# Token blocks of 512, 384 and 320 in place of 512, 480 and 320, in a fused attention and two-layer MLP kernel

## The chip, the cores and the metric

The kernel runs on one core of one Trainium2 chip. The metric is the device time of one execution in microseconds. A core has five engines with a queue of instructions each: TensorE (PE, matmuls), VectorE (DVE), ScalarE (ACT), GpSimd (POOL) and SyncE (SP, which issues nearly all DMA transfers here).

## The reference

Tokens `x` (12480 x 128, fp32) pass an induced-set attention with 32 inducing points, and then two MLP layers of width 2048. All is fp32.

```python
def mab(q, kv):
    s = scale * (q @ kv.transpose(0, 2, 1))
    s = s - s.max(-1, keepdims=True)
    a = np.exp(s)
    a /= a.sum(-1, keepdims=True) + 1e-09
    return a @ kv
h = mab(I, x)            # 32 x 128, over all tokens
x = mab(x, h)            # 12480 x 128

h = x @ w_in             # layer 1: 128 -> 2048
r = np.maximum(h, 0.0)
x = (s * (r * r) + b) @ w_out

h = x @ w_in2            # layer 2: 128 -> 2048
g = np.where(h >= 1, h, np.where(h <= -1, 0.0, (h + 1) ** 2 / 4))
out = g @ w_out2
```

## The kernel before

The tokens are cut into 25 blocks (`SIZES`): 20 of 512 tokens, four of 480 and one of 320. Tokens lie in a block as rows by parts: a block of `n` tokens is loaded as `n / 4` partitions with four tokens each (`KB = 4`), so a block of 480 is a load of 120 partitions and one of 320 a load of 80.

**First attention (the ramp).** Blocks go in groups of four (`g` = 0 to 6; group 5 holds blocks 20 to 23, group 6 block 24). SP loads them (`load_x`, tile `xc`). A group whose blocks have 120 rows is loaded as 112 rows for each block (L310) and one piece with the last 8 rows of all four (L308). PE transposes each block (`ptr`, L327), ACT copies it out (`x`, through a helper at L252), PE makes the scores of the four blocks side by side in one PSUM tile (`psc`, L344), DVE keeps a running maximum (`mx`, `m`, L350 to L358), ACT takes the exp (`e`, L364), PE transposes it (`pe`, L389), ACT copies (`eT`), and PE multiplies with the tokens (`ph`, L400) into the running sum `hsum`. `finish` makes `hT` of it, the 32 points of the second attention. Between these steps stands the conversion of the MLP weights, which come as 64-bit numbers (`raw_in`, `raw_out`, 512 KB a piece) and are made fp32 by ACT (`cvs`, an abs, L460) and DVE, and are then split in a high and a low fp32r part. Fillers (`warm`, `idle`) keep PE at work in planned gaps. SP's DMA instructions carry the waits of eight semaphores in turn, so each waits until the one eight places ahead has landed.

**Main loop.** A block has eight steps of two 128-wide slices of the hidden layer (`SPB = 8`, `GW = 2`); 25 blocks make 200 steps. A step `t` does layer 1 for step `t` and layer 2 for step `t - 18` (`LAG`). On PE it has 20 matmuls with the block's token count as columns: two of `in1` (`h`, L706), six of `out1` (`y`, L763 to L765), six of `in2` (`h`, L802 to L804) and six of `out2` (`y`, L763 to L765). Layer 1: ACT takes relu and square (L721, L728), POOL splits (`hi` L256, `lo` L738). Layer 2: DVE clips (`cl`, L809), ACT squares (L813), DVE adds (L820), ACT makes `hi` (L252), DVE makes `lo` (L830). `h2`, the PSUM tile of `in2`, has two buffers, and `lo` reads it, so `in2` of a step waits for `lo` of two steps before. At a block's end the result is transposed by DVE (`o`, L856) and stored by four DMAs (L860).

**Order.** The instructions of the ramp are emitted in the order of a list (`JOBS`) and of times that a planner (`Plan`) gives them by a table of costs. From step 26 to 192 the order is fixed by `ORDER`. From step 193 on the order comes from the list `LAST` (a letter is an operation, the number a step counted from 182), again through the planner; `EH` and `EL` set the engine of `hi` and `lo` for steps 175 to 181, and `TH` and `TL` for steps 182 to 199 (A is ACT, D is DVE, P is POOL). The last four steps of the last block skip the split and use a plain fp32 product (`out2_whole`, L847).

**Second attention.** For the MLP's input the scores of a group of up to four blocks (`sizes`) are taken with `hT` (L623), transposed by DVE, and turned into a softmax over some ten small operations of DVE, POOL and ACT that stand in the main loop, ahead of the blocks that need them.

Of the kernel before, what the change touches and what calls it, by code (L numbers as in the profile page):

```python
# [1306 lines left out]
```

## Time and profile before

| | |
|---|---|
| median of 3 runs | 940.8 us (938.71 to 940.96) |
| profiled execution | 942.43 us |
| its span in the trace | 940.6 us |
| PE busy | 921.8 us (98%) |
| ACT, DVE, POOL busy | 839.8, 808.3, 749.1 us |
| DMA | 28.13 MB moved; the packets of the main queue take 11.7% of the time of 16 engines |

The span is the time from the first to the last event of the core; the rest of the execution's time lies around it. The busy time of an engine is the time in which at least one of its instructions ran. Matmuls are pipelined and their ends are modelled, so what a matmul costs is read from the distance of the starts. "Idle before" stands in brackets behind an instruction, with what released it. The granted clock of PE is given as a share: 1.00 is 2.4 GHz and 0.50 is 1.2 GHz.

### The profile page before, as it was taken

The numbers are of one execution on the slowest core, as the hardware profiler recorded it, in microseconds if no ns is written. First come the engines' busy times: TensorE is split into PE (matmuls) and PEld (weight loads), VectorE is DVE, ScalarE is ACT, GpSimd is POOL, SyncE is SP. The second block draws the span as 40 slices with busy tenths as digits, with TensorE's granted clock in tenths as the row PEclk, the third lists the DMA queues.
The fourth block names the chain that finished last, engine by engine and source line by source line (L and its number), as shares of the span: only waits on it lengthen the run. The fifth ranks groups of instructions, "written<-read, shape, count | busy, mean of one in ns | idle before, by whom it ended". The sixth has DMA issues, their size and how long they took to land.

```text
span 940.6 us, 12488 instructions
## 1 busy us (share of the span) xinstructions
PE 921.8 (98%) x4540; PEld 779.7 (83%) x4540; DVE 808.3 (86%) x835; ACT 839.8 (89%) x911; POOL 749.1 (80%) x508
## 2 busy tenths in 40 slices
PE   8899999999999999999999999999999999999997
PEld 6654588888888888888888888888888888998986
DVE  6788988888898888898888888889888889888996
ACT  5658899999999999999999999999999999998874
POOL 0011389998999989999999899889999888997884
PEclk9999999999999999999999999999999999999999
DMA  9613000020001000002000002000110000000001
GB/s 336 207 45 90 0 1 13 12 45 12 1 12 43 15 12 12 1 11 53 7 9 12 7 5 46 12 1 12 20 35 12 11 1 13 19 1 11 11 12 18
DMA packets 64630, 28.13 MB, mean 30 GB/s; under 512 B 53224, under 2 KB 57992, under 8 KB 64568
## 3 DMA queue, kind: packets, MB, share of 16 engines
q1 hardware_dynamic: 64240, 27.28, 11.7%
q8 instruction: 36, 0.59, 0.3%
q14 instruction: 26, 0.21, 0.1%
q10 hardware_dynamic: 328, 0.04, 0.0%
HBM read 14.80 MB, written 6.39 MB: 23 GB/s over the span
## 4 chain that ended last, share of the span: by engine, by line
PE 92%; DMA 2%; ACT 2%; DVE 2%; issue 1%; SPq 0%; POOL 0%; ACTq 0%; DVEq 0%
PE y L763 17%; PE y L764 17%; PE y L765 17%; PE h L802 9%; PE h L804 9%; PE h L803 9%; PE h L706 9%; PE y L776 3%; DMA raw_out<-in_moe_w_out_dram 1%; DMA raw_in<-in_moe_w_in_dram 1%; ACT g L721 1%; ACT g L728 1%; PE ph L400 1%; DMA xc<-in_x_dram 0%; PE y L847 0%
## 5 line engine op out<-in xcount | busy, mean ns | idle before, releaser
L738 POOL TENSOR_TENSOR lo<-g,hi 128x1024 fp32r<-128x1024 f32 (+2 forms) x182 | 425.8, 2339 | 15.2
L809 DVE TENSOR_SCALAR cl<-h 128x1024 f32<-128x1024 f32 (+2 forms) x200 | 238.9, 1196 | 80.0 <-PE h L804 78.9
L763 PE MATMUL y<-hi,wout 128*128 128x512 f32 (+2 forms) x756 | 284.1, 376 | 0.9 <-DVE o L856 0.9
L764 PE MATMUL y<-lo,wout 128*128 128x512 f32 (+2 forms) x756 | 283.1, 374 | 0.3 <-POOL lo L830 0.3
L765 PE MATMUL y<-hi,wout 128*128 128x512 f32 (+2 forms) x756 | 282.9, 374 | 0.0
L813 ACT ACTIVATE cl<-cl,mhalf 128x1024 f32<-128x1024 f32 (+2 forms) x200 | 225.6, 1128 | 44.5 <-DVE cl L809 43.2
L256 POOL TENSOR_SCALAR hi<-g 128x1024 fp32r<-128x1024 f32 (+2 forms) x182 | 187.4, 1030 | 54.0 <-PE y L765 50.1
L820 DVE SCALAR_TENSOR_TENSOR h<-h,cl 128x1024 f32<-128x1024 f32 (+1 forms) x175 | 213.6, 1221 | 11.6 <-ACT cl L813 1.8
L830 DVE TENSOR_TENSOR lo<-h,hi 128x1024 fp32r<-128x1024 f32 (+1 forms) x175 | 211.9, 1211 | 8.0 <-ACT hi L252 7.6
L728 ACT ACTIVATE g<-g 128x1024 f32<-128x1024 f32 (+2 forms) x199 | 205.6, 1035 | 5.4
L721 ACT ACTIVATE g<-h 128x1024 f32<-128x1024 f32 (+2 forms) x198 | 195.2, 986 | 3.4 <-PE h L706 3.4
L252 ACT CAST hi<-h 128x1024 fp32r<-128x1024 f32 (+1 forms) x175 | 174.1, 995 | 1.3 <-DVE h L820 1.3
L763 PEld LDWEIGHTS y<-hi,wout 128*128 128x128 f32 x756 | 142.8, 189 | 22.4 <-issue 3.9
L764 PEld LDWEIGHTS y<-lo,wout 128*128 128x128 f32 x756 | 142.9, 189 | 18.0 <-POOL lo L830 0.7
L765 PEld LDWEIGHTS y<-hi,wout 128*128 128x128 f32 x756 | 142.9, 189 | 17.9
L802 PE MATMUL h<-y,win 128*128 128x512 f32 (+2 forms) x400 | 151.5, 379 | 1.8 <-DVE lo L830 1.2
L803 PE MATMUL h<-y,win 128*128 128x512 f32 (+2 forms) x400 | 149.5, 374 | 0.0
L804 PE MATMUL h<-y,win 128*128 128x512 f32 (+2 forms) x400 | 149.5, 374 | 0.0
L706 PE MATMUL h<-qt,hw 128*128 128x512 f32 (+2 forms) x400 | 119.8, 384 | 1.2 <-ACT g L721 0.9
L706 PEld LDWEIGHTS h<-qt,hw 128*128 128x128 f32 x400 | 74.9, 189 | 17.8 <-issue 4.7
L802 PEld LDWEIGHTS h<-y,win 128*128 128x128 f32 x400 | 75.5, 189 | 16.5 <-DVE lo L830 4.5
L804 PEld LDWEIGHTS h<-y,win 128*128 128x128 f32 x400 | 75.6, 189 | 9.5
(146 smaller groups left out, 648.1 us busy)
## 6 DMA issues: line engine op xcount, KB each, us to landing
xc<-in_x_dram SPq DMA_DIRECT2D x20, 256.0 KB
out_dram<-o SPq DMA_DIRECT2D x80, 64.0 KB
qin<-x SPq DMA_DIRECT2D x76, 64.0 KB
raw_in<-in_moe_w_in_dram SPq DMA_DIRECT2D x8, 512.0 KB
raw_out<-in_moe_w_out_dram SPq DMA_DIRECT2D x8, 512.0 KB
qin<-x SPq DMA_DIRECT2D x16, 60.0 KB
out_dram<-o SPq DMA_DIRECT2D x16, 60.0 KB
xc<-in_x_dram SPq DMA_DIRECT2D x4, 224.0 KB
```

The costliest lines, as they stand in the source:

```text
L706: nc.tensor.matmul(turned(p[:, j, :tb(bl)], bl), hw[f // 4][:, (f % 4) * 128:(f % 4 + 1) * 128], turns(qt[bl], bl), start=True, stop=True)
L728: nc.scalar.activation(g1[t], g1[t], AF.Square)
L738: engine[eng].tensor_sub(lo1[t], g1.pop(t), hi1[t].bitcast(F32))
L763: nc.tensor.matmul(p, whi, mhi, start=first, stop=False)
L764: nc.tensor.matmul(p, whi, mlo, start=False, stop=False)
L765: nc.tensor.matmul(p, wlo, mhi, start=False, stop=last)
L802: nc.tensor.matmul(o, whi, mhi, start=True, stop=False)
L803: nc.tensor.matmul(o, wlo, mhi, start=False, stop=False)
L804: nc.tensor.matmul(o, whi, mlo, start=False, stop=True)
L809: nc.vector.tensor_scalar(cl[t][:, part(js)], h2[t][:, part(js), :tb(t // SPB)], -1.0, 1.0, op0=ALU.max, op1=ALU.min)
L813: nc.scalar.activation(k, k, AF.Square, bias=mhalf, scale=0.5)
L820: nc.vector.scalar_tensor_tensor(oo[t][:, part(js)], h, -1.0, cl[t][:, part(js)], op0=ALU.max, op1=ALU.add)
```

## The change

The blocks become 23 of 512 tokens, one of 384 (block 23) and one of 320 (block 24). `SPAN` says how many partitions the last two are loaded to: 128 with three tokens each, and 64 with five each. The load of group 5 is thus four DMAs of 128 rows, without the 8-row piece. In group 5, whose other blocks have 512 columns, block 23 is treated as 512 columns wide: its spare columns are filled by transposing the first part again, and its spare scores are overwritten by a matmul of a row of ones with a row of -1e30. The parts of `e` and `ph` follow the new number of tokens a partition. In the second attention the scores of blocks 23 and 24 are written to PSUM in another order of columns, and the store of their results reads them in that order. `LAST`, `TH` and `TL` are new.

```diff
-SIZES = [TB] * 20 + [480] * 4 + [320]
+SIZES = [TB] * 23 + [384, 320]
+SPAN = {23: 128, 24: 64}
+MASK = -1e30
...
-TH = "AAADAAAAAAAAAAAAAA"
-TL = "PPPPPPPPPPPPPPPPPP"
+TH = "PAAAAAAAAAPAAAADAA"
+TL = "PDPPPPPDPPPPPPPPPP"
...
-    return SIZES[bl] // KB, KB, SIZES[bl], STARTS[bl]
+    tp = SPAN.get(bl, TP)
+    return tp, SIZES[bl] // tp, SIZES[bl], STARTS[bl]
...
+    ones = pre.tile([1, NM], F32, tag="ones", name="ones")
+    nc.vector.memset(ones, 1.0)
+    mask = pre.tile([1, 128], F32, tag="mask", name="mask")
+    nc.vector.memset(mask, MASK)
...
-                if whole < tp:
-                    xv = x[0][t0:t0 + len(blocks(g)) * n].rearrange("(i p k) c -> p i (k c)", p=tp, k=kb)
-                    nc.sync.dma_start(out=xc[g][whole:tp].rearrange("p (i k) c -> p i (k c)", k=kb), in_=xv[whole:])
-            xv = x[0][t0:t0 + n].rearrange("(p k) c -> p k c", k=kb)
-            nc.sync.dma_start(out=xc[g][:whole, i * KB:i * KB + kb, :], in_=xv[:whole])
+            nc.sync.dma_start(out=xc[g][:tp, i * KB:i * KB + kb, :],
+                              in_=x[0][t0:t0 + n].rearrange("(p k) c -> p k c", k=kb))
...
-                nc.tensor.matmul(ps[NM * i:NM * (i + 1), :cols], iT, xT[bl], start=True, stop=True)
+                nc.tensor.matmul(ps[NM * i:NM * (i + 1), :cols], iT, xT[bl][:, :cols], start=True, stop=True)
+                if tb(bl) < cols:
+                    nc.tensor.matmul(ps[NM * i:NM * (i + 1), tb(bl):cols], ones, mask[:, :cols - tb(bl)], start=True, stop=True)
...
+            if bl in SPAN:
+                v = v.rearrange("p (d k r) -> p k r d", d=16, k=n // SPAN[bl])
+            nc.tensor.matmul(v, hT[:, :NM], xT[bl][:, :n], start=True, stop=True)
+            if n < cols:
+                nc.tensor.matmul(o[:, n:cols], hT[:, :NM], xT[bl][:, n:cols], start=True, stop=True)
...
+        if bl in SPAN:
+            ov = out[t0:t0 + n].rearrange("(q t k) (r d) -> r t k q d", t=NM, k=kb, d=NM)
+            o = o.rearrange("p (k q) d -> p k q d", k=kb)
```

The order of instructions moves in few places. On SP, in the ramp, these stand between the loads of group 4 (`xc4`) and those of the weights of layer 2 (`raw_in20`) before; `raw_out1` to `raw_out3` are pieces of the second weight matrix of layer 1:

```order
L310 DMA xc4_323<-in_x_dram 128x512 x4
L446 DMA raw_out1_382<-in_moe_w_out_dram 128x4x256
L308 DMA xc5_405<-in_x_dram 8x4x512
L310 DMA xc5_405<-in_x_dram 112x512 x4
L446 DMA raw_out2_443<-in_moe_w_out_dram 128x4x256
L310 DMA xc6_477<-in_x_dram 80x512
L446 DMA raw_out3_518<-in_moe_w_out_dram 128x4x256
```

And these on SP, at the same place, in the changed kernel:

```order
L312 DMA xc4_327<-in_x_dram 128x512 x4
L452 DMA raw_out1_386<-in_moe_w_out_dram 128x4x256
L312 DMA xc5_402<-in_x_dram 128x512 x3
L312 DMA xc5_402<-in_x_dram 128x384
L452 DMA raw_out2_445<-in_moe_w_out_dram 128x4x256
L312 DMA xc6_462<-in_x_dram 64x640
L452 DMA raw_out3_519<-in_moe_w_out_dram 128x4x256
```

The 8-row piece is gone, and the rest stands in the same order with other row counts. On ACT, in the ramp, the exp of group 2 (`e2`) and the copies of blocks 20 to 23 (`x20` to `x22`, the last two blocks in one tile) stand so before:

```order
L364 ACTIVATE e2_486,l2_487<-psc2_325,nm2_457 128x512
L367 ACTIVATE al2_489<-m1_304,nm2_457 128x1
L252 COPY x20_79<-ptr20_448 128x480
L252 COPY eT2_513<-pe2_501 128x512
L460 ACTIVATE cvs_out2_516<-raw_out2_443 128x512
L252 COPY x21_80<-ptr21_479 128x480
```

And so on ACT, at the same place, in the changed kernel:

```order
L369 ACTIVATE e2_489,l2_490<-psc2_329,nm2_460 128x512
L372 ACTIVATE al2_492<-m1_308,nm2_460 128x1
L466 ACTIVATE cvs_out2_502<-raw_out2_445 128x512
L255 COPY eT2_517<-pe2_505 128x512
L255 COPY x20_79<-ptr20_451 128x512
L255 COPY x21_80<-ptr21_483 128x512
```

The abs of the weight piece `raw_out2` has moved two places forward, ahead of `eT2`, and the copy of block 20 behind it. On DVE, in the last part, steps 185 to 188 (`cl` the clip, `g1` the sum, `o22` the result of block 22) stand so before:

```order
L809 TENSOR_SCALAR cl_186_8575<-h2_186_8544 128x2x480
L809 TENSOR_SCALAR cl_187_8586<-h2_187_8568 128x2x480
L254 CAST hi2_185_8595<-g1_185_8562 128x2x480
L856 STREAM_TRANSPOSE o22_8600<-y2_22_8338 128x480
L820 SCALAR_TENSOR_TENSOR g1_186_8606<-h2_186_8544,cl_186_8575 128x2x480
L809 TENSOR_SCALAR cl_188_8616<-h2_188_8579 128x2x480
```

And so on DVE, at the same place, in the changed kernel:

```order
L821 TENSOR_SCALAR cl_186_8581<-h2_186_8549 128x2x384
L821 TENSOR_SCALAR cl_187_8592<-h2_187_8572 128x2x384
L842 TENSOR_TENSOR lo1_183_8595<-g1_183_8527,hi2_183_8579 128x1024
L832 SCALAR_TENSOR_TENSOR g1_186_8600<-h2_186_8549,cl_186_8581 128x2x384
L868 STREAM_TRANSPOSE o22_8610<-y2_22_8345 128x512
L821 TENSOR_SCALAR cl_188_8618<-h2_188_8585 128x2x384
```

`lo` of step 183 has come to DVE from POOL, and `hi` of step 185 has left it; `lo` of step 189 comes to DVE in the same way some ten places later.

## Rows read from the trace of the kernel before

**Rows 1.** Busy time by windows: us, busy time by engine, granted clock, DMA.
```profile
core 0: us, PE busy (x) PEld busy (x) DVE busy (x) ACT busy (x) POOL busy (x), PEclk, DMA share, GB/s
120.00:860.00 740.00, 740.00 (x3443) 646.65 (x3442) 644.27 (x577) 698.84 (x716) 673.86 (x449) 1.00 0.08 15
864.00:893.00 29.00, 29.00 (x163) 27.55 (x162) 26.80 (x24) 24.82 (x30) 22.90 (x17) 1.00 0.06 9
893.00:931.00 38.00, 36.25 (x201) 33.37 (x200) 33.71 (x37) 28.67 (x32) 31.87 (x17) 1.00 0.09 14
```

**Rows 2.** Timeline of PE: start us, duration us, instruction; main loop and last part.
```profile
500.01 0.38 PE L763 MATMUL y<-hi,wout 128*128 128x512 f32 x1
...
503.68 0.38 PE L765 MATMUL y<-hi,wout 128*128 128x512 f32 x1
...
925.27 0.30 PE L763 MATMUL y<-hi,wout 128*128 128x320 f32 x1
...
929.34 0.30 PE L763 MATMUL y<-hi,wout 128*128 128x320 f32 x1
```

**Rows 3.** The same windows in the ramp, where loads run.
```profile
20.00:25.00 5.00, 4.88 (x62) 3.37 (x63) 4.32 (x10) 4.01 (x11) 0.00 (x0) 1.00 1.07 397
25.00:26.00 1.00, 1.00 (x12) 0.74 (x14) 0.94 (x2) 1.00 (x3) 0.00 (x0) 1.00 1.13 103
26.00:30.00 4.00, 2.34 (x20) 1.27 (x12) 2.80 (x8) 1.13 (x4) 0.00 (x0) 1.00 1.06 260
31.50:33.00 1.50, 1.50 (x31) 1.12 (x24) 0.51 (x3) 1.34 (x5) 0.00 (x0) 0.64 0.15 34
34.00:38.50 4.50, 4.50 (x61) 3.28 (x60) 3.44 (x9) 2.92 (x6) 0.00 (x0) 0.85 1.06 391
```

**Rows 4.** Timeline of SP's queue: issue of the late piece and of the next.
```profile
19.89 0.38 SPq L446 DMA_DIRECT2D raw_out<-in_moe_w_out_dram  x1
20.42 0.34 SPq L308 DMA_DIRECT2D xc<-in_x_dram  x1
```

**Rows 5.** Timeline of ACT around the wait for the weight piece.
```profile
25.95 0.60 ACT L252 COPY x<-ptr 128x512 f32<-128x512 f32 x1
29.42 0.66 ACT L460 ACTIVATE cvs_out<-raw_out 128x512 f32<-128x512 f32 x1 [2.87 <-DMA raw_out<-in_moe_w_out_dram]
```

**Rows 6.** Timeline of PE around its gap in the ramp.
```profile
26.75 1.59 PE L327 MATMUL ptr<-ident,xc 128*128 128x128 f32 x12
30.61 0.63 PE L327 MATMUL ptr<-ident,xc 120*128 120x120 f32 x4 [2.26 <-ACT x L252]
...
32.37 1.86 PE L327 MATMUL ptr<-ident,xc 120*128 120x120 f32 x8
```

**Rows 7.** Timeline of PE at the end of the first attention.
```profile
46.47 1.06 PE L1126 MATMUL idle<-wz 128*128 128x128 f32 x8
...
50.01 1.06 PE L400 MATMUL ph<-xc,eT 80*32 80x128 f32 x8
```

**Rows 8.** Timeline of PE and DVE: a full step, and the stall.
```profile
503.94 1.21 DVE L830 TENSOR_TENSOR lo<-h,hi 128x1024 fp32r<-128x1024 f32 x1
...
505.62 0.38 PE L802 MATMUL h<-y,win 128*128 128x512 f32 x1
...
862.43 1.15 DVE L830 TENSOR_TENSOR lo<-h,hi 128x960 fp32r<-128x960 f32 x1
...
863.73 0.44 PE L802 MATMUL h<-y,win 128*128 128x480 f32 x1 [1.19 <-DVE lo L830]
```

**Rows 9.** Groups of DVE's clip by shape: count, busy us, mean ns, idle before.
```profile
L809 DVE TENSOR_SCALAR cl<-h 128x1024 f32<-128x1024 f32 x160 | 195.7, 1223 | 71.7 <-PE h L804 70.9
L809 DVE TENSOR_SCALAR cl<-h 128x960 f32<-128x960 f32 x32 | 36.9, 1154 | 8.3 <-PE h L804 8.0
...
L809 DVE TENSOR_SCALAR cl<-h 128x640 f32<-128x640 f32 x8 | 6.4, 817 | 0.0
```

**Rows 10.** Timeline of SP's queue at the end.
```profile
936.08 2.12 SPq L860 DMA_DIRECT2D out_dram<-o  x3
```

**Rows 11.** Busy time by windows, at the last store.
```profile
939.00:939.60 0.60, 0.00 (x0) 0.00 (x0) 0.00 (x0) 0.00 (x0) 0.00 (x0) 1.00 0.26 41
```

More of the change, by code (lines that the diff above doesn't have):

```diff
@@ L199, in moe_attn_kernel @@
         t = xts.tile([C, 1 + pair, TB], F32, tag=f"x{i}", name=f"x{i}")
-        xT += [t[:, k, :tb(i + k)] for k in range(1 + pair)]
+        xT += [t[:, k, :] for k in range(1 + pair)]
     hT = kt([C, 4 * NM], "hT")
@@ L321, in transposes, with on_pe @@
         for i, bl in blocks(g):
-            tp, kb, n, _ = tokens(bl)
-            def on_pe(i=i, bl=bl, tp=tp, kb=kb):
+            tp, kb, _, _ = tokens(bl)
+            n = tb(blocks(g)[0][1])
+            def on_pe(i=i, bl=bl, tp=tp, kb=kb, n=n):
                 T["tr", bl] = ptile("tr", f"ptr{bl}", TRB)
-                for k in range(kb):
-                    nc.tensor.transpose(T["tr", bl][:, k * tp:(k + 1) * tp], xc[g][:tp, i * KB + k, :], ident[:tp, :tp])
+                for k in range(n // tp):
+                    nc.tensor.transpose(T["tr", bl][:, k * tp:(k + 1) * tp], xc[g][:tp, i * KB + k % kb, :], ident[:tp, :tp])
             def evac(eng, bl=bl, n=n):
-                copy(eng, xT[bl], T.pop(("tr", bl))[:, :n])
-            t = add("PE", 0.11 * kb, on_pe, xd[g, i], P.get(("xT", bl - TRB)))
+                copy(eng, xT[bl][:, :n], T.pop(("tr", bl))[:, :n])
+            t = add("PE", 0.11 * (n // tp), on_pe, xd[g, i], P.get(("xT", bl - TRB)))
             P["tr", bl] = t
@@ L385, in tr @@
         def tr():
[L386 removed]
+            pe = T["pe", g] = pp.tile([128, TB], F32, tag="pe", name=f"pe{g}", bufs=1)
             e = T.pop(("e", g))
             for k in range(kb):
[L389 removed]
+                nc.tensor.transpose(pe[:tp, k * n:(k + 1) * n], e[:n, k * tp:(k + 1) * tp], ident[:n, :n])
         def evac(eng):
[L392 to L393 removed]
+            eT = T["eT", g] = pre.tile([TP, TB], F32, tag="eT", name=f"eT{g}", bufs=3)
+            copy(eng, eT[:tp, :kb * n], T.pop(("pe", g))[:tp, :kb * n])
         def on_pe():
@@ L398, in on_pe @@
             for k in range(kb):
-                for i, _ in blocks(g):
-                    nc.tensor.matmul(ph[NM * i:NM * (i + 1), :C], eT[:tp, k, NM * i:NM * (i + 1)],
-                                     xc[g][:tp, i * KB + k, :], start=(k == 0), stop=(k == kb - 1))
+                for i, bl in blocks(g):
+                    if k < tokens(bl)[1]:
+                        nc.tensor.matmul(ph[NM * i:NM * (i + 1), :C], eT[:tp, k * n + NM * i:k * n + NM * (i + 1)],
+                                         xc[g][:tp, i * KB + k, :], start=(k == 0), stop=(k == tokens(bl)[1] - 1))
         def total():
@@ L622, in soft_scores @@
             bl = first[g] + i
-            nc.tensor.matmul(ps[NM * i:NM * (i + 1), 0, :tb(bl)], hT[:, :NM], xT[bl], start=True, stop=True)
+            o, n, cols = ps[NM * i:NM * (i + 1), 0, :], tb(bl), tb(first[g])
+            v = o[:, :n]
+            if bl in SPAN:
[3 more added lines that the diff above has]
+                nc.tensor.matmul(o[:, n:cols], hT[:, :NM], xT[bl][:, n:cols], start=True, stop=True)
         sm[g, "s"] = ps
@@ L628, in soft_turn @@
         n, cols = NM * sizes[g], tb(first[g])
-        e = xT[first[g]][:n]
+        e = xT[first[g]][:n, :cols]
         sm[g, "e"] = e.rearrange("p (q j) -> p q j", j=NM)
@@ L670, in soft_move @@
                 nc.sync.dma_start(out=q[NM * r:NM * (r + 1), :],
[L671 removed]
+                                  in_=sm[g, "e"][NM * i:NM * (i + 1)].rearrange("p q j -> p (q j)")[:, :tb(first[g] + i)])
     def soft_q(bl):
```

22 lines of the change are left out of this document (8 added, 14 removed).

## The prediction

> **What bounds the kernel now.** I read the windows over the three long stretches first. TensorE (PE) is busy for 740.00 of 740 us between 120 and 860, and for 29.00 of 29 after that; no other engine reaches 95% there [rows 1]. So between the ramp and the last part the time is the number of matmul columns. The second reading is what a column costs: 17 matmuls of 512 columns start within 3.67 us, 0.2159 each, and 30 of 320 within 4.07 us, 0.1357 each [rows 2]. That is a line, 0.0017 us + 0.418 ns a column, and it gives 0.2024 at 480 and 0.1622 at 384. Time can therefore be gained or lost in three places only: the ramp before 120 us, where PE waits; the last part, where 1.75 us of the 38 between 893 and 931 are idle [rows 1]; and the five microseconds of stores at the end.
>
> The third reading is the ramp. There PE stands still for 2.26 us until 30.61, and is released by an ACT copy [rows 6]. ACT itself had waited 2.87 us, from the copy that ended at 26.55 to 29.42, with the abs of a weight piece (`cvs_out` from `raw_out`) at the head of its queue [rows 5]. That load was issued at 19.89 [rows 4]. Seven loads of 262 KB were ahead of it in flight, and it has 524 KB itself: 2.36 MB at the 397 GB/s of 20 to 25 us takes 5.9 us, so it was due at 25.8. It came 3.6 us late. In that time the rate was 103 GB/s from 25 to 26 and 260 from 26 to 30, with the engines just as busy (share 1.13 and 1.06); when 128-row loads run again it is 391 [rows 3]. What was issued just behind the late load is the 8-row piece, at 20.42 [rows 4], and then the four 112-row loads.
>
> **The change, part by part.**
>
> *Main loop: 0.* There are 25 blocks, 200 steps and 20 matmuls in a step before and after, and 12,480 columns. As the cost is a line in the columns, PE's sum does not change: what blocks 20 to 22 gain in columns, block 23 loses. It moves, though: the part after step 193 gets 2.4 us less of PE and the part before it as much more.
>
> *Loads: -2.26 and -1.3.* The 8-row and 112-row loads become three of 128 rows, one of 128 rows of 1536 bytes and one of 64 rows. If the 128-row rate (397) holds, the late piece lands at 25.8 to 26.5, before ACT reaches it at 26.55; block 20's rows (another 262 KB) land 0.7 us behind it, before PE has ended its transposes at 28.34 (26.75 + 1.59 [rows 6]). Then the whole 2.26 us goes. With it goes what followed the gap: the granted clock is 0.64 over 31.5 to 33, and 0.85 over 34 to 38.5 [rows 3], so the lower level, 1.2 GHz, held for 1.1 us, the 1.0 between the two windows and 1.35, about 3.4 us. Eight transposes took 1.86 us there, where twelve had taken 1.59, thus eight 1.06 [rows 6]: 43% of the time was lost. At that share 3.4 us lose 1.5; the price has 0.8 (these eight alone) as its lower end and 1.5 as its upper, and I take 1.3, since matmuls that wait for VectorE lose less. The moved `cvs_out`, now ahead of the copies of block 20, waits for the next piece. That piece is 0.98 + 0.52 MB further on, 3.8 us, due about 29.6. ACT gets there at about 29.8: the abs and two copies from 26.55, the third copy behind the transposes that end at 28.34, then an exp and a small one (0.9). So it costs nothing, and some 0.5 us if the piece is late, which then delays `eT`. The whole of what is bound here is 0 to -3.8.
>
> The Trainium skill, "DMA: Bandwidth & Descriptors", section "Why a DMA increments its semaphore by 16 and not by 1", gives the number of engines that one load uses as the largest divisor, up to 16, of the slowest dimensions: 8 rows get 8 engines, 112 rows get all 16, as 128 do. By that rule the 112-row loads should run at the rate of 128 rows, and only the 8-row piece (64 KB) is dear; the 260 GB/s above does not agree. It is the ground of the second rival.
>
> *Work added to the ramp: +0.7.* The mask is one more fp32 matmul of 128 columns on one group of 32 columns of the array: four pairs of 128 columns take 1.06 us [rows 7], so 0.26. `ph` of the last block gets five parts for four: eight records take 1.06 us [rows 7], so two more cost 0.26. 512 columns for 480 in one max, one exp and four copies cost about 0.03 each, some 0.2 of which lies on the chain. The two small memsets on VectorE, the fifth transposes and the mask columns of the later softmax lie beside idle time. Bounds 0.3 to 1.0.
>
> *The ring before the last part: +1.2.* In the loop `in2` of a step waits for `lo` of two steps before, which frees its PSUM. At 512 columns `lo` starts at 503.94, lasts 1.21, and `in2` starts at 505.62; when PE does wait, at 480 columns, it starts 0.15 after `lo` ends (862.43 + 1.15, 863.73) [rows 8]. So the ring clip, `lo`, `in2` has 0.47 - 0.15 = 0.32 us of slack in a step of 20 x 0.2159 = 4.32, and cannot turn faster than 4.00. In steps 184 to 191 `in1` and `out1` now have 384 columns and the other twelve matmuls still 512: 8 x 0.1622 + 12 x 0.2159 = 3.89. That is 0.11 too fast, eight times, less the slack once: 0.56; one store and one query transpose on VectorE fall into these steps and add up to 0.6 together. I take 0.9, bounds 0 and 1.5. At step 192 the kernel before already stalls for 1.19 us [rows 8]. There the ring grows by two VectorE operations of 1.223 for 1.154 [rows 9] and 0.08 of matmuls, and PE has a shorter `out1` to fill it: +0.3, bounds 0 and 0.5.
>
> *The last part: +0.2.* From 893 to 931 PE has 36.25 us of work and VectorE 33.71 [rows 1]. The change takes 8 x 12 x 0.0402 = 3.9 from PE and adds 0.3 for steps 182 and 183: 32.7. From VectorE it takes 16 operations x 0.20 (1.154 at 480 and 0.817 at 320 give 0.95 at 384 [rows 9]) = 3.3, and it adds two `lo` (1.2 and 0.95) for one `hi` of 0.7: 32.2. POOL is freed by the same two `lo`. So VectorE goes from 93% to 98% of PE. If all of PE's idle goes: -1.75. If VectorE waits as long as now (4.3 us): 36.5 for PE's 32.7 + 1.75, so +2.1. No row decides between the ends; I take their middle.
>
> *The end: -0.25.* The last stores begin to be issued at 936.08 [rows 10]; the last one moves its data behind 939.0, at 41 GB/s over 0.6 us, 25 KB of its 40 [rows 11]. Their shape changes from 8 to 160 rows and no row has that shape: between 0 and the 0.55 us in which data still move; I take about half.
>
> **Sum.** -2.26 - 1.3 + 0.7 + 0.9 + 0.3 + 0.2 - 0.25 = -1.7. The profiled execution took 942.43 (span 940.6 and 1.8 around it), so such a one takes 940.7; it lies 1.6 above the median of the runs shown, and so the median 940.8 becomes **939.1**.
>
> **Rivals.**
> 1. *The last part does better.* The ring's stalls are taken up by slack (0 for 1.2) and the new list leaves PE no idle (-1.75): -2.86 - 0.25 - 1.75 + 0.3 = -4.5, 936.3. For it: POOL, on which `out2` waits through `lo`, loses two of them. Against: VectorE gains them.
> 2. *The loads are not what was slow.* The change doesn't do what it says in DMA time; the weight piece itself (1 KB runs) is slow and still lands after 29. Then only +0.7 + 0.9 + 0.3 + 0.2 - 0.25 = +1.85 is left: 942.6. For it the page's rule on 112 rows; against it 391 GB/s with such pieces in flight [rows 3].
> 3. *VectorE becomes the bound from step 184 on.* Its ring at the dear end (1.5 + 0.5) and its idle in the last part unchanged (+2.1): 4.1 for the 1.4 in the sum, +1.0 in all: 941.8, slower than before. It decides from the point where what VectorE adds exceeds the ramp's 3.1. For it: 98% of PE; against it: PE never waits between 864 and 893 with VectorE at 26.80 of 29 [rows 1].
>
> **Chances.** My forecast 0.43, rival 1 0.26, rival 2 0.14, rival 3 0.17. A measurement here can tell about 0.3%, 2.8 us, from no change. The forecast's own range is 937.4 to 940.6, a quarter of it faster by more than that (0.11); rival 1 nearly all (0.25): faster 0.36. Rival 3 is slower by over 2.8 only if the ramp also gives little (0.05), rival 2 if the added work is at its upper ends (0.02): slower 0.07. Same is 0.57. The range goes from 936.2, just below rival 1, to 942.4, between rivals 3 and 2; about 0.08 is left out below and 0.1 above.
>
> **What would show it.** Loads: PE's idle before the first transposes of block 20 gone, the clock at 1.00 from 31 to 36, and about 400 GB/s from 25 to 29. Added work: the first main step earlier by some 2.9 us, and not by 3.6. Ring: PE idle before `in2`, released by VectorE's `lo`, in the 31 us ahead of the last part. Last part: PE's idle against 1.75. The forecast is wrong if the gap near 30 us stays, or if the gain of the ramp is not found again at 120 us because the conversions of weights on VectorE hold it.

## The result and the profile after

The changed kernel takes **950.65 us** (median of four, 949.75 to 951.86) where the kernel before took 939.96 (four runs on the same chip, 938.71 to 940.96). The ratio is 1.0115, 95% interval 1.0095 to 1.0136: slower, by a little over 1%. The prediction was 939.1 in a range of 936.2 to 942.4, a gain of 1.7; the step of it that failed is the one on the last part. The profiled execution took 951.44, its span is 949.7 (940.6 before).

The three stretches of [rows 1], as windows of the changed kernel:

```profile
120.00:860.00 740.00, 739.98 (x3428) 642.39 (x3427) 643.92 (x574) 697.93 (x713) 672.40 (x447) 1.00 0.08 15
864.00:893.00 29.00, 24.55 (x121) 21.53 (x120) 21.50 (x18) 19.19 (x23) 15.99 (x14) 0.94 0.06 10
893.00:931.00 38.00, 32.20 (x178) 28.87 (x177) 34.72 (x35) 26.65 (x31) 24.35 (x16) 1.00 0.05 8
```

The main loop is as full as before. From 864 to 893 PE, which had no idle there, is idle for 4.45 us, and the mean clock is 0.94; VectorE works 21.50 us for 26.80. An engine that becomes the bound would work more in such a stretch. Here both stand: they wait for each other.

Now PE's rows with idle ahead of them, from the switch to the end. The switch is the first `in2` of the list `LAST`, that of step 175, where the fixed `ORDER` ends; the prediction calls it step 192. A row has start, duration, line and names, and in brackets the idle and its releaser. Here eight stand behind the switch's, 8.68 us in all, where before four stood, with 1.76:

```profile
865.64 0.45 PE L814 MATMUL h<-y,win 128*128 128x512 f32 x1 [1.56 <-DVE lo L842]
...
871.73 0.45 PE L814 MATMUL h<-y,win 128*128 128x512 f32 x1 [0.71 <-DVE oe L832]
...
875.71 0.80 PE L814 MATMUL h<-y,win 128*128 128x512 f32 x1 [2.17 <-DVE lo L842]
...
894.43 0.45 PE L814 MATMUL h<-y,win 128*128 128x512 f32 x1 [1.22 <-DVE oe L832]
...
906.88 0.40 PE L814 MATMUL h<-y,win 128*128 128x384 f32 x1 [0.75 <-DVE g L832]
...
914.96 0.48 PE L776 MATMUL y<-lo,wout 128*128 128x512 f32 x1 [0.99 <-DVE lo L842]
...
917.11 0.43 PE L775 MATMUL y<-hi,wout 128*128 128x384 f32 x1 [0.81 <-DVE o L868]
...
921.23 0.43 PE L776 MATMUL y<-lo,wout 128*128 128x384 f32 x1 [0.76 <-POOL lo L842]
...
930.09 0.43 PE L776 MATMUL y<-lo,wout 128*128 128x384 f32 x1 [1.27 <-DVE lo L842]
```

What VectorE does around the first three (timeline of VectorE, changed kernel):

```profile
865.58 1.23 DVE L832 SCALAR_TENSOR_TENSOR h<-h,cl 128x1024 f32<-128x1024 f32 x1
867.22 1.23 DVE L821 TENSOR_SCALAR cl<-h 128x1024 f32<-128x1024 f32 x1 [0.41 <-PE h L816]
870.36 1.22 DVE L832 SCALAR_TENSOR_TENSOR oe<-h,cl 128x1024 f32<-128x1024 f32 x1 [1.92 <-ACT cl L825]
873.30 1.22 DVE L821 TENSOR_SCALAR cl<-h 128x1024 f32<-128x1024 f32 x1 [1.72 <-PE h L816]
874.44 1.21 DVE L842 TENSOR_TENSOR lo<-h,hi 128x1024 fp32r<-128x1024 f32 x1
875.57 1.22 DVE L842 TENSOR_TENSOR lo<-oe,hi 128x1024 fp32r<-128x1024 f32 x1
```

The first row is g2 of step 174, written in place into its PSUM tile (`h<-h`); it is the last step that does so, since from 175 on (`early`) g2 goes to SBUF (`oe`). Its `lo`, the reader that frees this tile for `in2` of step 177, comes at 874.44, behind the clip and g2 of 175 and the clip of 176. VectorE waits 1.92 and 1.72 us ahead of them, in which `lo` could have run (its `hi` is done on ACT at 867.91). In the kernel before the queue held clip 175, **`lo` 174**, g2 175, clip 176 (VectorE, kernel before):

```profile
865.22 1.16 DVE L809 TENSOR_SCALAR cl<-h 128x960 f32<-128x960 f32 x1 [0.37 <-PE h L804]
866.57 1.16 DVE L830 TENSOR_TENSOR lo<-h,hi 128x960 fp32r<-128x960 f32 x1 [0.20 <-ACT g L721]
868.29 1.16 DVE L820 SCALAR_TENSOR_TENSOR oe<-h,cl 128x960 f32<-128x960 f32 x1 [0.56 <-ACT cl L813]
870.35 1.16 DVE L809 TENSOR_SCALAR cl<-h 128x960 f32<-128x960 f32 x1 [0.91 <-PE h L804]
```

VectorE waited only 0.56 and 0.91 us ahead of g2 175 and clip 176 there, and PE not at all: its `in2` of step 176 started at 868.93, while g2 of 175 was still running, with `lo` 174 done at 867.73. In the changed kernel `in2` of 176 starts only 0.15 us behind the end of g2 175, and that of 177 only 0.06 behind the end of `lo` 174. So PE, ACT and VectorE work one after the other for two steps. Then the clock falls (windows of the changed kernel; behind the busy times of the five engines stand the granted clock, the DMA share and GB/s):

```profile
875.00:876.00 1.00, 0.29 (x1) 0.29 (x2) 1.00 (x2) 1.00 (x2) 0.00 (x0) 0.81 0.00 0
876.00:879.00 3.00, 3.00 (x9) 2.46 (x9) 2.24 (x3) 0.33 (x1) 0.00 (x0) 0.50 0.00 0
```

0.50 is the level of 1.2 GHz. Eight matmuls start from 876.30 to 878.96, five of 512 and three of 320 columns, and the next starts at 879.14: 2.84 us, where five at 0.2159 and three at 0.1357 [rows 2] are 1.49.

**The ring ahead of the last part** (VectorE, clip and `lo` of two steps):

```profile
855.12 1.22 DVE L821 TENSOR_SCALAR cl<-h 128x1024 f32<-128x1024 f32 x1
856.27 1.21 DVE L842 TENSOR_TENSOR lo<-h,hi 128x1024 fp32r<-128x1024 f32 x1
...
859.13 1.22 DVE L821 TENSOR_SCALAR cl<-h 128x1024 f32<-128x1024 f32 x1 [0.34 <-PE h L816]
860.27 1.21 DVE L842 TENSOR_TENSOR lo<-h,hi 128x1024 fp32r<-128x1024 f32 x1
```

The step is 4.01 us; the prediction had 4.00 against PE's 3.89.

**The ramp.** Windows that answer to [rows 3], then ACT's waits for the weight pieces [rows 5], then PE [rows 6]:

```profile
20.00:25.00 5.00, 5.00 (x68) 3.55 (x64) 4.72 (x10) 4.12 (x11) 0.00 (x0) 1.00 1.05 394
25.00:26.00 1.00, 1.00 (x11) 0.30 (x4) 0.95 (x2) 0.50 (x2) 0.00 (x0) 1.00 1.06 408
26.00:28.00 2.00, 2.00 (x24) 1.60 (x26) 1.91 (x7) 1.99 (x4) 0.00 (x0) 1.00 1.07 391
28.00:30.00 2.00, 2.00 (x43) 1.80 (x36) 1.81 (x6) 1.01 (x4) 0.00 (x0) 1.00 1.13 269
...
36.00:39.00 3.00, 3.00 (x17) 0.63 (x19) 1.28 (x4) 2.00 (x5) 0.00 (x0) 0.50 0.00 0
```

```profile
26.01 0.70 ACT L466 ACTIVATE cvs_out<-raw_out 128x512 f32<-128x512 f32 x1 [0.51 <-DMA raw_out<-in_moe_w_out_dram]
...
30.66 0.71 ACT L466 ACTIVATE cvs_out<-raw_out 128x512 f32<-128x512 f32 x1 [1.65 <-DMA raw_out<-in_moe_w_out_dram]
```

```profile
31.90 1.08 PE L406 MATMUL ph<-xc,eT 128*32 128x128 f32 x32 [0.55 <-ACT eT L255]
...
33.41 0.95 PE L974 MATMUL bsum<-b_sb,wo 128*128 128x1 f32 x8
34.29 0.52 PE L330 MATMUL ptr<-ident,xc 64*128 64x64 f32 x5
34.74 1.05 PE L974 MATMUL bsum<-b_sb,wo 128*128 128x1 f32 x8
...
36.43 1.93 PE L347 MATMUL psc<-x,iT 128*32 128x512 f32 x8
```

Up to 28 us the rate keeps at 391 to 408 GB/s, where it was 103 from 25 to 26 and 260 from 26 to 30; from 28 to 30 it is 269 here too. The late piece is there at 26.0 instead of 29.4, and the gap of 2.26 is gone. But the moved `cvs_out` waits to 30.66 and holds `eT` up by 0.55, and the clock is at 0.50 from 36 to 39, behind sixteen matmuls of one column (`bsum`). The last idle row of the ramp stands at 115.33 (116.76 before): 1.43 us, not 2.86.

**The end.** From the last transpose (944.97) to the end of the span it is 4.73 us, for 5.06 (935.54 to 940.60).

Four places in each trace make a table: the last idle row of the ramp, the `in2` at the switch, and the last transpose `o`. "Loop" and "tail" are the differences; these times are of one profiled execution each. Medians are in us; the ratio is to the kernel before on the same chip.

| kernel | ramp | switch | `o` | loop | tail | median | ratio (95%) |
|---|---|---|---|---|---|---|---|
| before | 116.76 | 863.73 | 935.54 | 746.97 | 71.81 | 939.96 | |
| changed | 115.33 | 865.64 | 944.97 | 750.31 | 79.33 | 950.65 | 1.0095-1.0136 |
| e1 `lo` 174 early | 114.03 | 864.35 | 937.93 | 750.32 | 73.58 | 944.42 | 1.0031-1.0060 |
| e2 old list | 115.20 | 865.52 | 947.65 | 750.32 | 82.13 | 953.72 | 1.0114-1.0160 |
| e3 old sizes, new list | 114.14 | 861.08 | 939.55 | 746.94 | 78.47 | 946.42 | 1.0046-1.0084 |
| e6 before, `lo` 174 late | 114.12 | 861.07 | 937.54 | 746.95 | 76.47 | 944.56 | 1.0023-1.0060 |
| e7 `lo` 178 on POOL | 113.94 | 864.28 | 937.73 | 750.34 | 73.45 | 944.52 | 1.0033-1.0063 |
| e8 before, whole loads | 112.87 | 859.86 | 931.77 | 746.99 | 71.91 | 939.62 | 0.9988-1.0007 |
| e9 `lo` 183 on POOL | 115.43 | 865.79 | 941.09 | 750.36 | 75.30 | 947.47 | 1.0061-1.0091 |
| e10 `bsum` late | 117.25 | 867.62 | 941.19 | 750.37 | 73.57 | 944.61 | 1.0034-1.0074 |
| e11 e1, no clip 176-191 | 115.11 | 865.47 | 939.53 | 750.36 | 74.06 | 945.62 | 1.0049-1.0076 |
| e12 `bsum` wide | 114.37 | 864.72 | 938.32 | 750.35 | 73.60 | 944.82 | 1.0041-1.0068 |
| e13 `bsum` late, wide | 115.52 | 865.91 | 939.48 | 750.39 | 73.57 | 944.50 | 1.0038-1.0066 |
| e14 e8, `bsum` wide | 114.10 | 861.05 | 932.87 | 746.95 | 71.82 | 938.98 | 0.9985-1.0004 |
| e15 e1, store later | 115.64 | 865.93 | 941.75 | 750.29 | 75.82 | 947.21 | 1.0047-1.0082 |
| e17 e15, no clip | 114.44 | 864.74 | 937.69 | 750.30 | 72.95 | 945.48 | 1.0036-1.0070 |
| e18 old list, both places | 115.69 | 865.98 | 943.33 | 750.29 | 77.35 | 948.75 | 1.0071-1.0103 |
| e19 order as before | 115.34 | 865.75 | 937.51 | 750.41 | 71.76 | 942.92 | 1.0017-1.0036 |
| e20 e19, no clip | 115.32 | 865.69 | 938.98 | 750.37 | 73.29 | 944.39 | 1.0025-1.0056 |
| e21 no clip from 168 | 113.95 | 862.15 | 932.04 | 748.20 | 69.89 | 939.27 | 0.9981-1.0001 |

The loop agrees within 0.12 us over all kernels of one set of sizes (but e21, which leaves out work there), so the table separates the parts cleanly. The ramp does not. Twelve kernels have the changed ramp as it is: in the profiles of four its last idle row stands at 113.9 to 114.4 us, and in those of eight, in which the clock falls to 0.50 at 36 to 37 us, at 115.1 to 115.7. A fall in the tail lengthens a tail in the same way; it is named below where it bears on a comparison.

### The profile page after: what moved, and what is told of

Same layout as the page of the kernel before. It is cut to its first block, busy times and chain, and to the rows that moved or that the text cites. A ratio compares the mean times of both kernels' runs of the same rounds, so it can differ in the third digit from the quotient of the medians.

```text
span 949.7 us, 12502 instructions
## 1 busy us (share of the span) xinstructions
PE 926.6 (98%) x4546; PEld 775.1 (82%) x4546; DVE 813.5 (86%) x838; ACT 839.9 (88%) x910; POOL 741.5 (78%) x508
## 4 chain that ended last, share of the span: by engine, by line
PE 88%; DVE 5%; DMA 3%; ACT 3%; issue 1%; SPq 0%; POOL 0%; ACTq 0%; DVEq 0%
PE y L776 16%; PE y L775 16%; PE y L777 16%; PE h L814 9%; PE h L718 8%; PE h L816 8%; PE h L815 8%; PE y L788 3%; DVE lo L842 1%; DMA xc<-in_x_dram 1%; DVE cl L821 1%; ACT g L733 1%; ACT g L740 1%; DMA raw_out<-in_moe_w_out_dram 1%; DVE oe L832 1%; DMA raw_in<-in_moe_w_in_dram 1%
## 5 line engine op out<-in xcount | busy, mean ns | idle before, releaser
L832 DVE SCALAR_TENSOR_TENSOR h<-h,cl 128x1024 f32<-128x1024 f32 x175 | 214.5, 1226 | 11.5 <-ACT cl L825 1.8
L842 DVE TENSOR_TENSOR lo<-h,hi 128x1024 fp32r<-128x1024 f32 x175 | 212.5, 1214 | 7.5 <-ACT hi L255 7.2
L255 ACT CAST hi<-h 128x1024 fp32r<-128x1024 f32 x175 | 175.3, 1002 | 1.4 <-DVE h L832 1.4
```

Source lines behind the costliest of these rows:

```text
L832: nc.vector.scalar_tensor_tensor(oo[t][:, part(js)], h, -1.0, cl[t][:, part(js)], op0=ALU.max, op1=ALU.add)
L842: engine[eng].tensor_sub(lo2[t][:, part(js)], oo[t][:, part(js)], hi2[t][:, part(js)].bitcast(F32))
```

## The experiments

The theory after the result: the loss is the place of `lo` 174 in VectorE's queue. Rivals: the sizes give VectorE too much to do wherever its work stands; or the new list does it.

**e1.** In `LAST`, on the changed kernel:

```diff
-i-7 n11 o-10 c-7 p11 u9 g-7 v9 o-9 i-6 c-6 h-8 l-8 n12
+i-7 n11 o-10 c-7 h-8 l-8 p11 u9 g-7 v9 o-9 i-6 c-6 n12
```

> The changed kernel with one edit: in the list of the last part, `h-8 l-8` stands before `g-7`, so that on VectorE `lo` of step 174 stands ahead of the g2 (`oe`) of step 175, as in the kernel before. The theory of the order: that `lo` frees the PSUM that `in2` of step 177 waits for; PE's idle of 0.71 at 871.73 and of 2.17 at 875.71 goes (2.9), with it the lower clock of 876 to 879 (3.4 us of matmuls at half rate, 1.5 lost), and perhaps the 1.22 at 894.43: 4.4 to 5.6 less than 950.7, so 945.1 to 946.3. The theory of the sizes (VectorE has too much to do with 512 columns, wherever its work stands): the idle only moves, 949 to 951. The theory of the list (the loss is in the newly searched list, by its lo on VectorE at 914.96 and 930.09): these stalls stay, and at most 3 us are gained.

944.42: 6.2 gained, somewhat more than expected, and the tail is 5.75 shorter (79.33 to 73.58). The idles at 871 and 875 are gone. The order theory holds, with 4 us left over. The edit moves more than `lo` 174: some operations of ACT and the store of block 21 change places behind it.

**e2 and e3** cross sizes and lists: the changed kernel with the old three tables, and the kernel before with the new ones.

> The changed kernel with TH, TL and LAST of the kernel before; sizes and loads as changed. On VectorE `lo` of step 174 still stands behind the clip of step 176, since the planner places it there with this list too; `lo` of 183 and 189 are back on POOL. Theory of the order: the stall at 871 to 879 stays, those at 914.96 (0.99), 917.11 (0.81) and 930.09 (1.27) go if they come from the list: 947.5 to 950.7. Theory of the list: back near the kernel before less what the ramp gained, 939 to 941. Theory of the sizes: 949 to 951.

> The kernel before with TH, TL and LAST of the changed one; sizes and loads as before. On VectorE `lo` of step 174 stands ahead of the g2 of step 175. Theory of the order: no stall of over 1.3 us at 865 to 880, the lower clock does not come; two more `lo` on VectorE in the last part cost 0 to 3: 940 to 943. Theory of the list: about 10 us more than before, 948 to 951. Theory of the sizes: 940, as before.

Both missed high: 953.72 and 946.42. The place of `lo` 174 comes with the sizes, not with the list (e2 has the stall, e3 does not), and on the new sizes the kernel is slower still with the old list, which settles the list theory for them. But each list is worse on the other's sizes. The new one costs 6.7 in the tail on the old sizes, where its `lo` of 183 and 189 on VectorE make PE wait 3.09 and 1.84, and the clock is at 0.50 from 905 to 911. The first of these rows of e3:

```profile
904.69 0.69 PE L764 MATMUL y<-lo,wout 128*128 128x480 f32 x1 [3.09 <-DVE lo L830]
```

The old one costs 2.8 more in the tail than the new one on the new sizes.

**e6**, the cross test on the kernel before, one line ahead of the planner's call for `lo`:

```diff
+        d += 0.3 if u == tail[0] - 8 else 0.0
```

> The kernel before with one edit: the planner's cost of `lo` of step 174 is 0.3 us higher, so that it stands on VectorE behind the g2 of step 175 and the clip of step 176, as in the changed kernel; sizes, loads and lists as before. Theory of the order: PE stalls there as in the changed kernel (about 2.9 of idle where 0 was, and 1.5 through the clock): 3 to 6 us slower than 940.0, so 943 to 946. Theories of the sizes and of the list: 940 to 941, since neither is changed here.

944.56: the expected 943 to 946. Tail 76.47 for 71.81. The same picture on old sizes (VectorE, then PE):

```profile
865.62 1.16 DVE L820 SCALAR_TENSOR_TENSOR oe<-h,cl 128x960 f32<-128x960 f32 x1 [1.91 <-ACT cl L813]
868.42 1.16 DVE L809 TENSOR_SCALAR cl<-h 128x960 f32<-128x960 f32 x1 [1.64 <-PE h L804]
869.50 1.15 DVE L830 TENSOR_TENSOR lo<-h,hi 128x960 fp32r<-128x960 f32 x1
```

```profile
870.70 0.47 PE L802 MATMUL h<-y,win 128*128 128x480 f32 x1 [2.04 <-DVE lo L830]
```

This `lo` is the only instruction that has another place in e6, on any engine, from the switch to the end. One moved instruction of 1.15 us costs 4.7 us in the tail, 4.2 in the medians. Part of it is the clock: it falls in all three profiles with `lo` 174 late (changed, e2, and e6, where it is 0.50 from 873 to 875), and at this place in no other. The run also suggests why `lo` moved with the new sizes, which is not shown further: the planner's costs grow with the columns (`us`), a dearer `lo` no longer fits ahead of g2 175, and the plan does not know that it frees a PSUM tile. At this place it makes `in2` wait only for g2 of two steps before.

**e7, e9** take work from VectorE in e1: `EL = "DDDPDDP"`, and `TL = "PPPPPPPDPPPPPPPPPP"`.

> The kernel of the run with `lo` of step 174 early (944.4), with one edit more: EL is DDDPDDP, so `lo` of step 178 runs on POOL (2.38 us for 1.21 on VectorE). Theory that VectorE is the bound in steps 176 to 183 (three operations of 1.21 to 1.23 a step and a store's transpose, for 3.68 of PE): PE's idle of 1.28 at 888.75, released by VectorE's g2, goes or falls below 0.5; 943.0 to 943.8. Rival, that PE there waits for the order and not for VectorE's sum: the idle stays or moves to `out2` of step 178, released by POOL: 944.4 to 946.

> The kernel of the run with `lo` of step 174 early (944.4), with one edit more: TL is PPPPPPPDPPPPPPPPPP, so `lo` of step 183 is back on POOL. Theory that it stands badly on VectorE (behind two clips there, while POOL has 1.8 us idle): PE's 0.99 before `out2` of step 183 goes, and VectorE is 1.2 earlier behind it: 942.6 to 943.7. Rival, that POOL is then as full as VectorE (with all `lo` on POOL PE waited 1.47 and 2.03 for POOL in the run of the old list): 944.0 to 946.

e7: the idle of 1.28 falls to 0.82, the time does not. e9: 1.7 us longer in the tail, and 947.47 is beyond both expectations; the 0.99 goes, and PE waits 1.19 for g2 and 1.47 for a `lo` of POOL. Taking single operations from VectorE gives nothing.

**e8** on the kernel before: `whole = tp` for `whole = tp // 16 * 16`.

> The kernel before with one edit: each block of 480 is loaded in one DMA of 120 rows, not in 112 and a joint piece of 8. Theory that the 8-row piece is what is slow: the rate from 25 to 30 us is near 390 GB/s, as with 128 rows, PE's gap before the transposes of block 20 (2.26 and in two other runs 1.5) falls below 0.5: 939.0 to 940.0. Theory that loads with fewer than 128 rows are slow whether split or not: the rate stays below 300, the gap stays: 940 to 941.

939.62, ratio 0.9998: no change. The rate is between the two (window of e8):

```profile
26.00:30.00 4.00, 3.30 (x53) 2.65 (x50) 3.04 (x10) 2.91 (x8) 0.00 (x0) 1.00 1.04 297
```

So loads of 120 rows are slow without the 8-row piece too, but not as slow as with it: the gap shrinks to 0.70, from 1.49 and 1.53 in e3 and e6.

**e10, e12, e13, e14** ask about the ramp. `bsum` is 32 matmuls of one column, from 33.4 to 62.7 us in the changed kernel. e10 lets them wait for `st`, the first matmul that needs `hT`; e12 (on e1), e13 (on e10) and e14 (on e8) give each 128 equal columns:

```diff
-        nc.tensor.matmul(T["bsum"][:, :1], ..., b_sb, ...)
+        nc.tensor.matmul(T["bsum"][:, :128], ..., b_rep, ...)
```

> The kernel of the run with `lo` of step 174 early (944.4), with one edit more: the sixteen matmuls of one column (`bsum`, eight records of 0.9 us twice between 33 and 36 us, and eight at 41) run behind the first matmul that needs hT, where PE has fillers. Theory that PE's own work sets the ramp from 31 to 41 us: hT 1.5 to 2.0 earlier, 942.4 to 943.0. Rival, that the chain through ACT and VectorE sets it: hT not over 0.5 earlier, 944.0 to 944.6. And of the clock: if the granted clock falls in the ramp because of these matmuls, it is 1.00 from 36 to 41 here; if it falls although they are gone, something else sets it off.

> The kernel of the run with `lo` of step 174 early (944.4; five executions between 943.9 and 945.9), with one edit more: each matmul of `bsum` has 128 equal columns for one (some 0.13 us for 0.11, so 0.2 more in the ramp). Theory that PE, though busy without a break, falls to the lower clock because of the one-column matmuls at 33 to 36 us (in the profiles of three of five kernels with the changed ramp it fell right behind them, for 3 to 4 us): 1.00 from 35 to 41 us, and all executions within 1 us, 943.8 to 944.6. Rival, that the clock falls there for another reason: the executions still spread over 2 us, and the clock falls in the profile or not as before.

> The kernel of the run with `bsum` behind hT (five executions: 943.6, 943.9, 944.6 and 947.7, 947.8; in the profiled one the clock fell at 52 us, 1.3 us after 16 one-column matmuls in a row had begun, and stayed low to 62), with 128 equal columns for one in each of these matmuls. Theory of the one-column matmuls: the clock is 1.00 from 50 to 63 us, and no execution is at 947: 943.4 to 944.4. Rival, that it falls for another reason: executions near 947 still come, or the clock falls in the profile.

> The kernel before with 120-row loads in one DMA (939.6) and `bsum` in 128 equal columns; sizes and lists as before. If the clock's falls in the ramp come from the one-column matmuls here too: 938.6 to 939.4, faster than 939.9 by 0.1%, and executions within 1 us. If those in this kernel come from PE's gap before block 20 (0.7 in the last profile): 939.6 as with the whole loads alone.

e10: `hT` is used at 49.66 for 49.98. PE waits 1.23 and 1.73 us for ACT's exp instead; the rival was right, the chain through ACT and VectorE sets the ramp from 31 us on. In e10's profile the clock keeps at 1.00 from 36 to 41 and falls behind the moved matmuls, at 52. e12: the clock stays at 1.00, but the executions spread over 1.35 us and the median is 0.4 higher. e13: no execution near 947, but in its profile the clock is at 0.50 from 44 to 46, behind those waits. e14: 0.9995, not told apart from the kernel before. What sets off the clock's falls in the ramp is not settled by this.

**e11** (on e1) takes the clip of steps 176 to 191 away:

```diff
-        nc.vector.tensor_scalar(cl[t][:, part(js)], h2[t]..., -1.0, 1.0, op0=ALU.max, op1=ALU.min)
+        if not 176 <= t < 192:
+            nc.vector.tensor_scalar(cl[t][:, part(js)], h2[t]..., -1.0, 1.0, op0=ALU.max, op1=ALU.min)
...
-        nc.scalar.activation(k, k, AF.Square, bias=mhalf, scale=0.5)
+        nc.scalar.activation(k, src, AF.Square, bias=mhalf, scale=0.5)
```

> The kernel of the run with `lo` of step 174 early (944.4), which leaves out the clip of steps 176 to 191 (ACT squares straight from PSUM), so that VectorE has two operations a step there for three; order, sizes and PE's work as there. Theory that VectorE's sum is what is left of the loss: PE's idle behind 880 (1.28, 0.99, 0.81, 0.78 and 1.27, 5.1 in all) falls below 2: 940.5 to 942. Rival, that what is left are the places in the list and POOL's part: at least 4 of the 5.1 stay: 943.5 to 945.

945.62, tail 74.06: a third of VectorE's work gone there and nothing gained. Its trace shows VectorE waiting 3.03 us for a store's transpose, ahead of `lo` 176. e15 puts that transpose back behind g2 177, e17 leaves out the clip as well, e18 has the old list with both places right:

```diff
-            P["store", u // SPB] = add("DVE", 0.57, lambda: store(u // SPB), P["out2", u])
+            after = P.get(("g2", u + 2)) if u == tail[0] - 7 else None
+            P["store", u // SPB] = add("DVE", 0.57, lambda: store(u // SPB), P["out2", u], after)
```

> The kernel of the run with `lo` of step 174 early (944.4), with one edit more: the planner lets the store's transpose of block 21 wait for the g2 of step 177, so that on VectorE it stands behind `lo` of 176 and g2 of 177, as in the kernel before (it stood ahead of both and waited 1.52 us for `out2` of step 175, with them behind it). Theory of the order: PE's idle of 1.28 at 888.75 goes or falls below 0.3, the rest of the tail unchanged: 942.9 to 943.5. Theory that VectorE has too much to do with 512 columns: at least 1.0 of it stays, here or behind: 944.0 to 945.

> As the run with the store later, and the clip of steps 176 to 191 left out as in the run without clip (945.6, with an idle of 1.06 and VectorE waiting 3.03 for that transpose). If VectorE's amount of work still costs something in steps 176 to 191 once the order is as before, this is faster than the run with the store later by more than 1 us (below 942); if only places cost, the idle near 889 is 0 in both and they differ by less than 1 us.

> The changed sizes with the old TH, TL and LAST, with `lo` of step 174 early and the store of block 21 later, thus with VectorE's order of the kernel before up to step 185. Tail from the switch to the last transpose: 82.1 with the old list as it was, less 5.75 for `lo` of 174 and 1.3 for the store, about 75.1, and 72.3 for the new list with both: so 945 to 947.5 if the new list is worth 2.8 on the new sizes; 942.5 to 944 if it is worth nothing once both places are right.

My expectation of e15 fell: 947.21, tail 75.82, 2.2 worse than e1. 1.3 of that is there at `in2` of step 188; the rest comes while the clock is at 0.50, from 914 to 916, which it is not in e1. The transpose had hidden a wait for ACT (VectorE in e15):

```profile
879.60 1.92 DVE L842 TENSOR_TENSOR lo<-oe,hi 128x1024 fp32r<-128x1024 f32 x1 [2.15 <-ACT hi L255]
```

e1's edit had also moved `hi` 176 on ACT behind the square of step 177. Counted from the switch, e17 is 1.6 ahead of e15 at `in2` of step 188 and 2.9 better over the whole tail, 1.7 in the medians; e18 is 1.5 worse, with no fall of the clock in its tail. So in this disturbed order amount does cost, and the new list is worth 1.5 or more. With four executions each the medians alone would not tell these kernels apart surely. None of e11, e15, e17 and e18 came out in a range that was expected.

**e19** restores ACT too, so both engines stand as in the kernel before over steps 174 to 185; **e20** and **e21** are e19 without the clip of 176 to 191, and of 168 to the end.

```diff
-o-8 h-7 c-5 h-6 l-6
+o-8 h-7 h-6 l-6 c-5
```

> The kernel of the run with the store later (947.2), with one edit more: `h-6 l-6` stands before `c-5` in the list, so that on ACT `hi` of step 176 stands ahead of the square of step 177, as in the kernel before (it had come to stand behind it with `lo` of 174 early, and `lo` of 176 waited 2.15 us for it). With this ACT and VectorE have the order of the kernel before from step 174 to 185. Theory of the places: PE's idle before 900 (0.85, 0.63) goes, and the tail from the switch to the last transpose is 71 to 73 us (75.8 with the store later, 73.6 with `lo` of 174 early alone, 71.8 in the kernel before): 942 to 943.5. Theory that VectorE has too much to do: the tail stays at 73.5 or more, 944 to 947.

> The same with the clip of steps 176 to 191 left out. With the order as before, what this is faster by is what VectorE's amount of work costs in these steps: by the theory of the places under 1 us, by that of the amount 2 to 4.

> The same with the clip left out from step 168 to the end, the eight steps before the last part (the ring clip, `lo`, `in2`, 4.01 us a step for 3.89 of PE, and the 1.56 at the switch) and the last block included. If VectorE's amount of work is what is left of the loss, this reaches the kernel before or less (938 to 940.5), and the switch has no idle over 0.5. If it does not reach 941, places and the chain from step to step hold the rest.

e19: 942.92 (ten executions), as the theory of the places expected. The tail is 71.76, that of the kernel before (71.81), which has 2.4 more of columns there. VectorE's queue around step 175:

```profile
867.32 1.23 DVE L821 TENSOR_SCALAR cl<-h 128x1024 f32<-128x1024 f32 x1 [0.40 <-PE h L816]
868.74 1.23 DVE L842 TENSOR_TENSOR lo<-h,hi 128x1024 fp32r<-128x1024 f32 x1 [0.20 <-PE y L776]
870.47 1.23 DVE L832 SCALAR_TENSOR_TENSOR oe<-h,cl 128x1024 f32<-128x1024 f32 x1 [0.51 <-ACT cl L825]
872.45 1.23 DVE L821 TENSOR_SCALAR cl<-h 128x1024 f32<-128x1024 f32 x1 [0.75 <-PE h L816]
```

e20: 944.39, no gain, so with the order right VectorE's amount in steps 176 to 191 costs little. Up to `in2` of step 188 PE is no earlier than in e19, and from 189 to 194 it is 0.8 ahead, as the 0.99 before `out2` of 183 goes. Then it loses that and 1.5 more: `lo` 189 takes 2.27 us for 1.31 and ends when it did in e19, PE waits 2.12 for 1.27, and the clock is at 0.50 from 924 to 927. e21: 939.27. The loop is 2.2 shorter and the switch has

```profile
862.15 0.48 PE L814 MATMUL h<-y,win 128*128 128x512 f32 x1 [0.22 <-DVE lo L844]
```

so the ring and the switch are VectorE's amount, as the prediction had them, and so is a part of the last block. None of these kernels is measurably faster than the kernel before.

## Why the prediction was wrong, step by step

| term | predicted | measured |
|---|---|---|
| loads, clock, added work | -2.86 | -1.43 in the two profiles; -0.1 where the clock fell in neither |
| ring and switch | +1.2 | +0.9 (loop +3.3, of which 2.4 are moved columns) |
| last part | +0.2 (-1.75 to +2.1) | +9.9 (tail +7.5, where 2.4 of columns left) |
| end | -0.25 | -0.3 |

With the -1.43 of the two profiles for the ramp the measured column adds up to 9.1, the difference of the spans.

- **Last part: the step that failed.** The sum weighed VectorE's and PE's work (32.2 for 32.7 us; the terms that it names give 31.9) and took the waits as between none and as before. That holds only while the order holds. VectorE's order had changed at step 174 too, ahead of the steps 185 to 188 that the section on the change lists. The prediction doesn't mention it: no term and no bound had a price for a moved release of a PSUM tile. 7.6 of the 9.9 are that order (79.33 to 71.76, e19; 7.7 in the medians), 5.75 with `lo` 174 put back (e1); `lo` 174 alone costs 4.7 on the old sizes (e6). The other 2.3, a little over the upper bound of 2.1, go with the waits for `lo` 183 and 189 (0.99 and 1.27 in e19) and with what VectorE has to do at the end: without the clip 1.9 of it goes (e21).
- **Ring: right**, mechanism and size (4.01 us a step; 1.56 at the switch for 1.19; gone in e21). The two rows of the line give 0.0020 us and not 0.0017 as its constant, which moves no term by 0.05.
- **Loads: the mechanism was right, the size was not.** The 128-row rate held and the gap went. But 2.26 and the fall of the clock belonged to the one profiled execution: e3 and e6 have the same ramp, with gaps of 1.49 and 1.53 and no fall behind them. Their ramp ends at 114.14 and 114.12; that of e1, changed and without a fall, at 114.03 (last idle rows of e3 and e1):

```profile
114.14 0.70 PE L706 MATMUL h<-qt,hw 128*128 128x512 f32 x2 [0.24 <-ACT g L721]
```

```profile
114.03 0.70 PE L718 MATMUL h<-qt,hw 128*128 128x512 f32 x2 [0.24 <-ACT g L733]
```

  That the profiled execution lay 1.6 us above the median was the sign; I carried the 1.6 over as a constant. The added work cost about twice the 0.7: from the transposes at 26.5 to those of `e` (`pe`, at 35.88 in e1 and 36.84 in e3) e1 takes 0.56 longer than e3 without its gap of 1.49, and from there to the last idle row, with the mask and the longer `ph`, 0.85.
- **Rivals.** The first was wrong: PE's idle in the last part grew from 1.76 to 8.68. The second (loads not the reason) was wrong on the rate and on the piece, which was there at 26.0. The third had the sign and named the ring's place rightly, but what cost most in the last part was not VectorE's amount: from 864 to 893 it worked 21.50 of 29 us.
- **The sum with the ramp of e1 and e3**: 0.9 + 9.9 - 0.3 - 0.1 is 10.4, and the medians differ by 10.7.

## What to carry to other kernels

Where a change alters the costs that a planner places by, go through every row that moved on the in-order engines and ask what the moved instruction frees: a 1.15 us operation that releases a buffer cost 4.7 us by standing two places later (e6), which no sum of busy times shows. Give a stall the price that several executions show, and be wary when the profiled one lies above the median. Restoring one place can move others (e1 moved `hi` on ACT): check the order on all engines before a rival is read from the result.

## What the runs showed of the hardware

- The clock can fall while PE is busy without a break. In e2 PE is busy 11.00 of 11 us from 26 to 37 at a granted clock of 1.00, with sixteen matmuls of one column from 33.5 on, and the clock is 0.50 from 37 to 40. It need not fall: in e1, with the same matmuls, it is 1.00 from 32 to 42. In e10 sixteen one-column matmuls begin at 50.57; PE has been busy since 49.66, behind an idle of 0.38 (windows of e10):

```profile
51.00:52.00 1.00, 1.00 (x11) 1.00 (x10) 0.93 (x4) 0.14 (x1) 1.00 (x2) 0.97 0.49 94
52.00:62.00 10.00, 10.00 (x31) 5.28 (x31) 6.85 (x13) 1.91 (x4) 2.29 (x2) 0.50 0.12 43
```

  It stays at 1.2 GHz for 10 us, with PE busy 10.00 of 10. The Trainium skill, "TensorE: Matmul & The Clock Gate", section "HAM oscillation — how this bites in real kernels", warns of idle gaps of PE; in e2 the fall came without one.
- VectorE's `lo` of 1.21 us takes 1.92 when it starts (878.02 in e1) while a `lo` of POOL runs (877.31 to 878.86). The Trainium skill, "SBUF — State Buffer", section "Who interferes with whom", says that an operation of VectorE with two inputs in SBUF contends with a reading one of GpSimd for a shared port, and that the order of issue decides which of the two blocks; `oe` and `hi` are in SBUF, and waiting until 878.86 would add an estimated 0.84, near the 0.71 of the row.
- With loads of 120 rows in flight the rate was 264 GB/s from 25 to 26 us and 297 from 26 to 30, against 388 from 20 to 25, with loads of 128 rows ahead of them (e8). In the changed kernel, with 128 rows, the same windows have 408 and 330; weight pieces and the shorter load of block 24 are in flight in them too. By the Trainium skill, "DMA: Bandwidth & Descriptors", section "Why a DMA increments its semaphore by 16 and not by 1", 120 rows use 15 of 16 engines, which would be an estimated 364 by the 388; the windows of e8 lie below that, with the other loads in them.
